# Low halves one form behind on GpSimd, one addition behind on VectorE, forms made at named places, and a broadcast copy moved from VectorE to ScalarE

## The chip, the cores and the metric

The kernel runs on one core of one Trainium2 chip. The metric is device microseconds for one execution of the whole program, as a median of runs. The engines are named as in the profile: PE is TensorE's matmul (PEld its weight load), DVE is VectorE, ACT is ScalarE, POOL is GpSimd, SP is the queue that issues the DMAs. Each engine works through its own queue in order and waits for the others through semaphores.

## What is computed

Block-causal attention over 4 batches, 8 heads, 576 positions, then a mixture of experts whose gate is balanced by eight rounds of row and column normalisation, then a soft mixture of experts:

```
x = attention(q, k, v)                      # 2304 x 512
logits = x @ w_gate
P = exp(logits - logits.max())
for _ in range(8):
    P /= P.sum(1, keepdims=True) + 1e-9
    P /= P.sum(0, keepdims=True) + 1e-9
    P *= N / E
for e in range(8):
    h = maximum(x @ w1[e], 0)               # 512 -> 1024
    out += P[:, e:e+1] * (h @ w2[e])        # 1024 -> 512
return soft_moe(out, phi, m2w1, m2w2)
```

## The kernel before

A product in full precision is made of three matmuls on rounded operands: high by high, high by low, low by high, where the high half is a rounded copy made by ACT and the low half is the source minus that copy, made by DVE or POOL. So each operand has two halves, and the low half waits for the high one.

The 8 experts are cut into 32 units u of 256 hidden columns each. Units 0 to 3 run between the attention steps. While unit 4 runs, sums and differences of the tokens are built once (`rec`, `lin`, `form`). From unit 5 on, layer 1 for the four token chunks of 512 is done by a fast multiplication: 26 products instead of 32, each of a token form with a weight form, and sums of the products. The list `IR` sets the order of these 26 products and of the copies and additions that belong to them; every product goes to one of six PSUM banks. The last chunk of 256 tokens goes the plain way (`L1P`, chunk 4, 24 matmuls of 256 columns).

Weight forms: a unit has 26, numbered k. The first 8 are blocks of the raw weight tile `r1`; the other 18 are a sum or difference made by POOL in a scratch tile (`st`, `st2`). `make()` makes the next one of the queue `aq`: POOL's sum (L902, for k of 8 and over), ACT's high half (L903), POOL's low half (L904). It is called after every piece of layer 1 (`inter` calls it while `MAIN` is set), eight times at a hook, and by `wt_of` when a product needs a form that is not there. The calls pin the order on POOL and on ACT (`keep`).

One unit goes so: the 26 products (`L1S`, matmuls at L963) are interleaved with pieces of layer 2 of the unit before and of chunk 4. Layer-2 pieces are three matmuls at L203, and a bank of six of them is added to the output by DVE at L213 (`acc`). ACT copies banks at L966, DVE adds a bank to a work tile at L970, POOL adds two work tiles, also at L970. A "fin" step makes the two halves of a hidden tile through `hsplit`: ACT's relu at L923, DVE's low half at L924. Then come layer 2 of chunks 0 and 1, and the next unit. The raw w2 tile is split by ACT (L120) and DVE (L121) in the same stretch.

The gate: `gmax_a` finds the maximum of each partition, spreads it over 128 columns (L303), PE transposes that, and `gmax_b` takes the maximum and the exponential and goes on into the first normalisation:

```
nc.vector.tensor_reduce(out=m1, in_=o[:, 0:128], axis=AX.X, op=ALU.max, negate=True)   # L308
nc.scalar.activation(out=P, in_=P, func=AF.Exp, bias=m1, scale=1.0)                    # L309
nc.vector.tensor_reduce(out=rs, in_=P, axis=AX.X, op=ALU.add)                          # L313
nc.vector.tensor_scalar(out=rs, in0=rs, scalar1=1e-9, scalar2=None, op0=ALU.add)       # L314
nc.vector.reciprocal(out=rs, in_=rs)                                                   # L315
nc.vector.tensor_tensor(out=P, in0=P, in1=rs..., op=ALU.mult)                          # L316
nc.vector.tensor_reduce(out=cs, in_=P..., axis=AX.X, op=ALU.add)                       # L317
```

The next column sum (L322, on PE) needs `cs`. At that time POOL builds the token sums: 48 additions of 128 by 512 (L795).

Of the kernel before, what the change touches and what calls it, by code (L numbers as in the profile page):

```python
# [10 lines left out]
AF = mybir.ActivationFunctionType  # L11
# [18 lines left out]
def f32(ap):  # L30
    return ap.bitcast(F32)
# [3 lines left out]
def attn_moe_softmoe_kernel(ctx: ExitStack, tc: tile.TileContext, qk1, q, k, v, wg, w1, w2, phi, m2w1, m2w2, cst, out):  # L35
# [264 lines left out]
    def gmax_a():  # L300
        nc.vector.tensor_reduce(out=m1, in_=P, axis=AX.XY, op=ALU.max)
        mbt[0] = wp.tile([128, 128], F32, tag="r", name="mbg", bufs=RB)
        nc.vector.tensor_copy(out=mbt[0], in_=m1.to_broadcast([128, 128]))  # L303

    def gmax_b():
        o = bank("gm")
# [476 lines left out]
    k = 0  # L783
# [7 lines left out]
    def keep(ins):  # L791
        tc.keep_in_program_order(ins)
# [44 lines left out]
    def raw_w2(u):  # L837
        def f():
            e, fq = divmod(u, F // FQ)
            pool, tag = (pb, "hC1") if u == 4 else (wp, "r")  # L840
            rw2[u] = pool.tile([128, 2, DM], F32, tag=tag, name="r2")
            nc.sync.dma_start(out=rw2[u], in_=w2[e, fq * FQ:(fq + 1) * FQ, :].rearrange("(k p) f -> p k f", p=128))
        return [f]

    def split_w2(u):
        i = ND + u - 4

        def new():
            wslot[i % 2] = (None, None) + tuple(wp.tile([128, 2, DM], F32R, tag=f"{n_}{i % 2}", name=n_) for n_ in ("w2h", "w2l"))
            wraw[i % 2] = (None, rw2[u])  # L850
            split_piece(i, 4)
        return [new] + [lambda pc=pc: split_piece(i, pc) for pc in range(5, 8)]
# [22 lines left out]
    def unit(u, k):  # L875
        return rw[u][:, k % 4, 128 * (k // 4):128 * (k // 4) + 128]

    def forms_of(u, plain, last):
        for k in range(26):
            n = PA.count(k) * (not plain) + (k < 8) * (5 if plain else 1)  # L880
            if n:
                eu[u, k] = n
                aq.append((u, k))

    def make():
        if not aq or not efree:
            return
        u, k = aq.pop(0)
        q = efree.pop(0)
        h, lo = entry(q)  # L890
        ew[u, k] = (h, lo, q)
        if k < 8:
            src = unit(u, k)
        else:
            if not tmpw:
                tmpw.extend([const.tile([128, 512], F32, tag="wgx", name="st"), const.tile([128, 128], F32, name="st2")])
            d, ka, a, kb, b, o = AT[k - 8]

            def tv(j):
                return tmpw[j // 4][:, 128 * (j % 4):128 * (j % 4) + 128]  # L900
            src = tv(d)
            keep(nc.gpsimd.tensor_tensor(out=src, in0=unit(u, a) if ka == "u" else tv(a), in1=unit(u, b) if kb == "u" else tv(b), op=ALU.add if o == "+" else ALU.subtract))  # L902
        keep(nc.scalar.activation(out=h, in_=src, func=AF.Copy))  # L903
        keep(nc.gpsimd.tensor_tensor(out=lo, in0=src, in1=f32(h), op=ALU.subtract))  # L904

    def make_all(u):
        while aq and aq[0][0] == u:
            assert efree
            make()

    def wt_of(u, k):
        while (u, k) not in ew:
            assert efree
            make()
        return ew[u, k][0:2]

    def used(u, k):
# [4 lines left out]
    def hsplit(h, lo, src, pin=False):  # L922
        p = [nc.scalar.activation(out=h, in_=src, func=AF.Relu)]  # L923
        p.append(nc.vector.scalar_tensor_tensor(out=lo, in0=src, scalar=0.0, in1=f32(h), op0=ALU.max, op1=ALU.subtract))  # L924
        for x in p if pin else ():
            keep(x)
# [7 lines left out]
    def L1S(u, hb):  # L934
        bk, wk = {}, {}

        def v(q):
            if q[0] == "b":
                return bk[q[1]]
            _, t, f, k = q  # L940
            if t == 4:
                return w4
            if (t, k) not in wk:
                p, g = HT[t][k == "l"]
                wk[t, k] = p.tile([128, 2, H_], F32, tag=g, name="wk")
            return wk[t, k][:, f]
        r = []
        for o in IR + [("mm",)]:
            if o[0] == "y":
                yield  # L950
            elif o[0] == "mm":
                if r:
                    yield
                if len(o) == 1:
                    break
                r.append(o)
                _, n, b, st = o
                if st:
                    bk[b] = pm2.tile([128, 512], F32, tag=f"n{b}", name="s")
                wh, wl = wt_of(u, PA[n])  # L960
                xhv, xlv = XF[n]
                for m, (a, x) in enumerate(((wh, xhv), (wh, xlv), (wl, xhv))):
                    nc.tensor.matmul(bk[b], a, x, start=(st and m == 0), stop=(m == 2), skip_group_check=not st)  # L963
                used(u, PA[n])
            elif o[0] == "copy":
                keep(nc.scalar.activation(out=v(("s",) + o[1]), in_=v(o[2]), func=AF.Copy, scale=float(o[3])))  # L966
            elif o[0] in ("add", "addb"):
                out_ = v(("s",) + o[1]) if o[0] == "add" else bk[o[1]]
                ps_ = o[2][0] == "b" or o[3][0] == "b"
                keep((nc.vector if ps_ else nc.gpsimd).tensor_tensor(out=out_, in0=v(o[2]), in1=v(o[3]), op=ALU.add if o[4] == "+" else ALU.subtract))  # L970
            else:
                t, f = o[1]
                if t not in hb:
                    hb[t] = h_new(t, F32R, "hf")
                hsplit(hb[t][0][:, f], hb[t][1][:, f], v(o[2]), True)

    def L1P(c, u, hs):
        hh, hl = hs
        n = CH[c]
        for f in range(2):  # L980
            o = bank("l1")
            for kt in range(KD):
                wh, wl = wt_of(u, 4 * f + kt)
                xhv, xlv = xs(xh, c, kt), xs(xl, c, kt)
                nc.tensor.matmul(o[:, 0:n], wh, xhv, start=(kt == 0), stop=False)
                nc.tensor.matmul(o[:, 0:n], wh, xlv, start=False, stop=False)
                nc.tensor.matmul(o[:, 0:n], wl, xhv, start=False, stop=(kt == KD - 1))
                used(u, 4 * f + kt)
                if kt == KD - 1:
                    hsplit(hh[:, f, 0:n], hl[:, f, 0:n], o[:, 0:n])  # L990
                yield

    def inter(g1, pend, pat, at=None, part=False):
        g2 = (y for x in pend for y in L2(*x))
        n = 0
        for ch in pat:
            next(g1 if ch == "p" else g2, None)
            if ch == "p":
                pop_side()
                if MAIN[0]:  # L1000
                    make()
                n += 1
                for f in (at or {}).get(n, ()):
                    f()
        for g in (g2,) if part else (g2, g1):
            for _ in g:
                pass
# [29 lines left out]
    for j, x in enumerate(["3", "2", "1", "0", "4"]):  # L1037
        if j == 1:
            while side:
                pop_side()  # L1040
        h = (hB, hA)[(j + (pend[0][2] == hB if j == 0 else flip)) % 2]
        if j == 0:
            flip = int(pend[0][2] == hB)
        n2 = 2 * (ITEM[pend[0][1]][2] // 128)
        inter(L1P(int(x), 4, h), pend, PP[n2])
        pend = [(ND, x, h)]
        if x != "4":
            assert len(gated) == NC_
            aux.extend(batch(int(x)))
        if j == 2:  # L1050
            aux.extend(raw_w2(5) + split_w2(5) + dma_w1(5))
    drain()
    apace[0] = 1
    MAIN[0] = 1
# [22 lines left out]
    for u in range(5, NU - 1):  # L1077
        i = ND + u - 4
        h4 = h_new(0, F32R, "h4")
        if u > 5:  # L1080
            inter(L1P(4, u, h4), [(i - 1, "2", hb[2])], "llll" + "p" * 8 + "llll")
            late_ = [(i - 1, "3", hb[3])]
        else:
            inter(L1P(4, u, h4), pend, "ll" + PP[4].replace("l", "", 2))
            late_ = []
        at = {17: [lambda: make_all(u)] + raw_w2(u + 1)}
        after = dma_w1(u + 1)[0]

        def l2s(hb):
            for c in range(2):  # L1090
                yield from L2(i, str(c), hb[c])
        hb = stage_s(
            u, [(i, "4", h4)] + late_, "lplplplp" + ("plppl" * 3 + "plplp" + "p" * 10 if late_ else "p" * 22), at,
            l2s, "llllyllyllyllyl", {2: split_w2(u + 1), 15: [after] + [make] * 8},
        )

    u = NU - 1
    last_i = ND + u - 4
    lp = last_i % 2
    for _ in L2(last_i - 1, "2", hb[2]):  # L1100
        pass
    h4 = []

    def last_p(hb):
        t = pb.tile([128, 2, 2, 256], F32R, tag="T12", name="h4")
        h4.extend([t[:, 0], t[:, 1]])
        return L1P(4, u, h4)
    hb = stage_s(u, [(last_i - 1, "3", hb[3])], "plppl" * 4 + "p" * 14, {}, last_p, "ppppypypypypp", {})
    assert not aq and not aux

    A = const.tile([128, DM], F32, tag="wgx", name="A")
# [405 lines left out]
```

## Time and profile before

| | |
|---|---|
| median of 3 runs | 2041.64 us (2039.04 to 2050.18) |
| profiled execution: its time, its span | 2047.44 us, 2045.7 us |
| busy: PE, DVE, POOL, ACT | 1835.8, 1229.0, 1016.5, 787.6 us |
| longest shares of the chain that ended last | PE 32%, POOL 28%, DVE 21%, issue 10%, ACT 7% |
| POOL low halves and sums in that chain (L904, L902) | 11% and 8% |
| load of a raw weight tile (512 KB), issue to landing | 3.4 us |

Busy time is the share of the span in which an engine had something to do; a busy PE is not a PE at its peak. In the chain that ended last each piece of work is followed back to what released it, so its shares tell who was waited for, not who was busy.

### The profile page before, as it was taken

Reading aid. Unit: us, or ns where it says so; the run is one execution under the profiler, and the core shown is the slowest. Engines: PE = TensorE matmul, PEld = TensorE weight load, DVE = VectorE, ACT = ScalarE, POOL = GpSimd, SP = SyncE. Lnnn points to the kernel's source line nnn. Section 1 sums busy time; section 2 is a strip of 40 time slices with the busy share of each in tenths; the row PEclk is TensorE's granted clock in tenths of the full one; section 3 lists DMA queues with packets and bytes.
Section 4 is the critical chain, followed back from the end, with each engine's and each line's share of the span. In section 5 each row is a group of like instructions: output and inputs, shape, how many; then the busy total and the mean of one; then the engine's idle time right before and its main releaser. Section 6 shows DMA issues by size and latency. Waiting matters only on the chain.

```text
span 2045.7 us, 27013 instructions
## 1 busy us (share of the span) xinstructions
PE 1835.8 (90%) x9138; PEld 1368.5 (67%) x9138; DVE 1229.0 (60%) x2286; ACT 787.6 (39%) x2196; POOL 1016.5 (50%) x1706
## 2 busy tenths in 40 slices
PE   9999998399788889888989899889888889988897
PEld 5666666387566667666767677667666667666563
DVE  6565555876566666666666666666666666666442
ACT  6666552135333333333333333333333333333332
POOL 4332225711555565566665555555555555555511
PEclk9999999699899999999999999999999999999999
DMA  5333210010000000000000000000000000000687
GB/s 200 105 103 95 66 54 11 21 52 1 21 21 21 21 21 21 21 22 21 12 21 21 21 21 13 20 21 21 21 21 21 21 21 21 21 21 22 227 280 248
DMA packets 79066, 103.14 MB, mean 50 GB/s; under 512 B 4688, under 2 KB 55632, under 8 KB 78928
## 3 DMA queue, kind: packets, MB, share of 16 engines
q1 hardware_dynamic: 78928, 101.42, 14.8%
q8 instruction: 73, 1.20, 0.2%
q14 instruction: 65, 0.53, 0.1%
HBM read 96.68 MB, written 4.72 MB: 50 GB/s over the span
## 4 chain that ended last, share of the span: by engine, by line
PE 32%; POOL 28%; DVE 21%; issue 10%; ACT 7%; POOLq 0%; DMA 0%; ACTq 0%; DVEq 0%
PE l L203 13%; POOL es L904 11%; POOL st L902 8%; POOL wk L970 5%; DVE s L970 5%; DVE wk L970 4%; DVE acc L213 4%; POOL w L970 3%; DVE hf L924 3%; ACT hf L923 3%; DVE w2l L121 2%; PE pvp L531 2%; DVE mbg L303 2%; PE tp L499 2%; PE s L417 2%
## 5 line engine op out<-in xcount | busy, mean ns | idle before, releaser
L203 PE MATMUL l<-w2h,hf 128*128 128x512 f32 x1728 | 588.6, 395 | 9.3 <-DVE acc L213 7.5
L963 PE MATMUL s<-xh,es 128*128 128x512 f32 x864 | 340.9, 416 | 63.5 <-DVE hf L924 28.1
L970 POOL TENSOR_TENSOR wk<-wk 128x512 f32<-128x512 f32 x189 | 244.4, 1311 | 305.1 <-DVE wk L970 305.0
L213 DVE SCALAR_TENSOR_TENSOR acc<-l,P,acc 128x512 f32<-128x512 f32 x504 | 362.9, 743 | 54.9 <-PE l L203 54.8
L203 PEld LDWEIGHTS l<-w2h,hf 128*128 128x128 f32 x1728 | 324.9, 188 | 95.6 <-DVE acc L213 18.5
L203 PE MATMUL l<-w2l,hf 128*128 128x512 f32 x864 | 338.0, 391 | 0.0
L904 POOL TENSOR_TENSOR es<-st,es 128x128 fp32r<-128x128 f32 x486 | 223.6, 460 | 211.6 <-ACT es L903 205.1
L903 ACT ACTIVATE es<-st 128x128 fp32r<-128x128 f32 x486 | 150.9, 311 | 456.8 <-POOL st L902 454.9
L963 PE MATMUL s<-T,es 128*128 128x512 f32 x810 | 229.0, 408 | 48.6 <-DVE wk L970 41.7
L963 PEld LDWEIGHTS s<-xh,es 128*128 128x128 f32 x864 | 165.4, 192 | 149.4 <-DVE hf L924 48.9
L923 ACT ACTIVATE hf<-s 128x512 fp32r<-128x512 f32 x189 | 110.1, 597 | 396.1 <-DVE s L970 241.5
L970 DVE TENSOR_TENSOR wk<-s,wk 128x512 f32<-128x512 f32 x216 | 148.4, 687 | 156.9 <-POOL wk L970 55.2
L963 PEld LDWEIGHTS s<-T,es 128*128 128x128 f32 x810 | 149.2, 192 | 107.2 <-DVE wk L970 59.3
L203 PEld LDWEIGHTS l<-w2l,hf 128*128 128x128 f32 x864 | 162.6, 188 | 30.8
L963 PE MATMUL s<-xl,es 128*128 128x512 f32 x432 | 172.1, 398 | 0.0
L904 POOL TENSOR_TENSOR es<-r,es 128x128 fp32r<-128x128 f32 x224 | 95.7, 464 | 144.2 <-ACT es L903 144.2
L924 DVE SCALAR_TENSOR_TENSOR hf<-s,hf 128x512 fp32r<-128x512 f32 x189 | 129.9, 688 | 43.6 <-ACT hf L923 40.8
L970 DVE TENSOR_TENSOR wk<-wk,s 128x512 f32<-128x512 f32 x81 | 55.7, 688 | 126.1 <-POOL w L970 90.4
L970 DVE TENSOR_TENSOR s<-s,wk 128x512 f32<-128x512 f32 x162 | 111.8, 690 | 26.0 <-POOL wk L970 23.1
L475 POOL TENSOR_SCALAR pe<-pe,sm 128x384 f32<-128x384 f32 (+2 forms) x80 | 54.1, 680 | 142.3 <-DVE sm L462 64.0
L203 PE MATMUL l<-w2h,h 128*128 128x512 f32 x216 | 87.4, 406 | 30.4 <-ACT h L923 16.3
L924 DVE SCALAR_TENSOR_TENSOR h<-l,h 128x256 fp32r<-128x256 f32 x54 | 22.9, 424 | 149.1 <-ACT h L923 149.1
(247 smaller groups left out, 3189.3 us busy)
## 6 DMA issues: line engine op xcount, KB each, us to landing
r<-in_moe_w_dram SPq DMA_DIRECT2D x80, 512.0 KB, 3.4
mw<-in_moe_w_dram SPq DMA_DIRECT2D x64, 512.0 KB, 6.4
kraw<-in_k_dram SPq DMA_DIRECT2D x16, 576.0 KB, 4.1
qraw<-in_q_dram SPq DMA_DIRECT2D x16, 320.0 KB, 4.7
v<-in_v_dram SPq DMA_DIRECT2D x16, 256.0 KB, 3.1
out_dram<-ob SPq DMA_DIRECT2D x6, 512.0 KB, 4.0
out_dram<-ob SPq DMA_DIRECT2D x6, 256.0 KB, 2.3
qk<-in_qk_dram SPq DMA_DIRECT2D x4, 256.0 KB, 4.4
```

What stands on the lines that cost most here:

```text
L121: p.append((nc.gpsimd if pc % (2 if i >= ND_ - 2 else WPM) == 0 and (i < WPU or ND_ - 2 <= i <= ND_) else nc.vector).tensor_tensor(out=lo, ...
L203: nc.tensor.matmul(o, lh, w[:, kf, :], start=(m == 0), stop=(m == 5))
L213: nc.vector.scalar_tensor_tensor(out=av, in0=o, scalar=P[:, tt, e:e + 1], in1=av, op0=ALU.mult, op1=ALU.add)
L303: nc.vector.tensor_copy(out=mbt[0], in_=m1.to_broadcast([128, 128]))
L475: nc.gpsimd.tensor_scalar(out=p_[:, 0:n_], in0=p_[:, 0:n_], scalar1=sm[:, i:i + 1], scalar2=1.0, op0=ALU.mult, op1=ALU.mult)
L902: keep(nc.gpsimd.tensor_tensor(out=src, in0=unit(u, a) if ka == "u" else tv(a), in1=unit(u, b) if kb == "u" else tv(b), op=ALU.add if o == ...
L903: keep(nc.scalar.activation(out=h, in_=src, func=AF.Copy))
L904: keep(nc.gpsimd.tensor_tensor(out=lo, in0=src, in1=f32(h), op=ALU.subtract))
L923: p = [nc.scalar.activation(out=h, in_=src, func=AF.Relu)]
L924: p.append(nc.vector.scalar_tensor_tensor(out=lo, in0=src, scalar=0.0, in1=f32(h), op0=ALU.max, op1=ALU.subtract))
L963: nc.tensor.matmul(bk[b], a, x, start=(st and m == 0), stop=(m == 2), skip_group_check=not st)
L970: keep((nc.vector if ps_ else nc.gpsimd).tensor_tensor(out=out_, in0=v(o[2]), in1=v(o[3]), op=ALU.add if o[4] == "+" else ALU.subtract))
```

## The change

1. `gmax_a` makes the spread copy on ACT.
2. `make()` no longer makes the low half at once. It notes it in `owed`; the next `make()` puts it behind its own sum. `wt_of`, `make_all` and a scratch tile that is needed again put out what is owed.
3. The "fin" step of `L1S` puts ACT's relu out and notes the low half in `late`; it is put out behind the next addition from a bank, or ahead of a product that opens a bank.
4. `inter` calls `make()` where the pattern has an "m", no longer after every piece of layer 1. Around chunk 4 the calls stand between pieces of layer 2 and none stands between its eight pieces of layer 1; unit 5's first eight forms are queued in unit 4. The split of chunk 4 is pinned in its place, and the hook that loads the next raw w1 stands at piece 3 instead of 15.

```diff
     def gmax_a():
-        nc.vector.tensor_copy(out=mbt[0], in_=m1.to_broadcast([128, 128]))
+        nc.scalar.activation(out=mbt[0], in_=m1.to_broadcast([128, 128]), func=AF.Copy)
...
+    owed = []
+    def flush_lo():
+        while owed:
+            out_, src_, h_, _ = owed.pop(0)
+            keep(nc.gpsimd.tensor_tensor(out=out_, in0=src_, in1=f32(h_), op=ALU.subtract))
     def make():
...
+            if any(x[3] == d for x in owed):
+                flush_lo()
             keep(nc.gpsimd.tensor_tensor(out=src, in0=unit(u, a) if ka == "u" else tv(a), in1=unit(u, b) if kb == "u" else tv(b), op=ALU.add if o == "+" else ALU.subtract))
+        flush_lo()
         keep(nc.scalar.activation(out=h, in_=src, func=AF.Copy))
-        keep(nc.gpsimd.tensor_tensor(out=lo, in0=src, in1=f32(h), op=ALU.subtract))
+        owed.append((lo, src, h, d))
...
+            if o[0] == "y" or len(o) == 1 or o[0] == "mm" and o[3]:
+                flush()
...
                 keep((nc.vector if ps_ else nc.gpsimd).tensor_tensor(out=out_, in0=v(o[2]), in1=v(o[3]), op=ALU.add if o[4] == "+" else ALU.subtract))
+                if ps_:
+                    flush()
...
-                hsplit(hb[t][0][:, f], hb[t][1][:, f], v(o[2]), True)
+                h_ = hb[t][0][:, f]
+                keep(nc.scalar.activation(out=h_, in_=v(o[2]), func=AF.Relu))
+                flush()
+                late.append((hb[t][1][:, f], v(o[2]), h_))
...
-                    hsplit(hh[:, f, 0:n], hl[:, f, 0:n], o[:, 0:n])
+                    hsplit(hh[:, f, 0:n], hl[:, f, 0:n], o[:, 0:n], MAIN[0])
...
-                if MAIN[0]:
-                    make()
...
+        if j == 3:
+            aux.extend([make] * 8)
...
-            inter(L1P(4, u, h4), [(i - 1, "2", hb[2])], "llll" + "p" * 8 + "llll")
+            inter(L1P(4, u, h4), [(i - 1, "2", hb[2])], "lmlmlml" + "p" * 8 + "lmlmlmlm")
...
-            l2s, "llllyllyllyllyl", {2: split_w2(u + 1), 15: [after] + [make] * 8},
+            l2s, "llllyllyllyllyl", {2: split_w2(u + 1), 3: [after], 15: [make] * 8},
```

How instructions move is seen in the order of the built program, for one unit in the middle. On POOL, in the stretch in which chunk 4 is at work, before (`es` are the weight forms, `r1` the raw tile, `st` the scratch tile):

```order
L902 TENSOR_TENSOR st_5498<-r1_9209 128x128
L904 TENSOR_TENSOR es0_4990<-st_5498,es0_4990 128x128 [waits PE_49,Activation_49]
L902 TENSOR_TENSOR st2_5499<-r1_9209 128x128
L904 TENSOR_TENSOR es1_5025<-st2_5499,es1_5025 128x128 [waits PE_49,Activation_49]
L902 TENSOR_TENSOR st_5498<-st2_5499,r1_9209 128x128
L904 TENSOR_TENSOR es0_4990<-st_5498,es0_4990 128x128 [waits PE_49,Activation_49]
```

The same place after the change:

```order
L912 TENSOR_TENSOR st_5462<-r1_9164 128x128
L890 TENSOR_TENSOR es3_5405<-st_5462,es3_5405 128x128 [waits PE_49,Activation_49]
L912 TENSOR_TENSOR st2_5463<-r1_9164 128x128
L890 TENSOR_TENSOR es0_4990<-st_5462,es0_4990 128x128 [waits PE_49,Activation_49]
L912 TENSOR_TENSOR st_5462<-st2_5463,r1_9164 128x128 [waits Pool_49]
L890 TENSOR_TENSOR es1_5024<-st2_5463,es1_5024 128x128 [waits PE_49,Activation_49]
```

Each low half now belongs to the sum before the one in front of it: a sum stands between a sum and its low half.

On ACT, around the second relu of chunk 4 (`h4<-l1`), before:

```order
L903 ACTIVATE es0_4990<-st_5498 128x128 [waits Pool_49]
L903 ACTIVATE es1_5025<-st2_5499 128x128 [waits Pool_49]
L903 ACTIVATE es0_4990<-st_5498 128x128 [waits Pool_49]
L903 ACTIVATE es3_5474<-st_5498 128x128 [waits Pool_49]
L923 ACTIVATE h4_9247<-l1_9292 128x256 [waits PE_49]
L903 ACTIVATE es1_5025<-st2_5499 128x128 [waits Pool_49]
```

After:

```order
L914 ACTIVATE es3_5405<-st_5462 128x128 [waits PE_49,Pool_49] x2
L937 ACTIVATE h4_9246<-l1_9273 128x256 [waits PE_49]
L937 ACTIVATE h4_9246<-l1_9288 128x256 [waits PE_49]
L914 ACTIVATE es0_4990<-st_5462 128x128 [waits Pool_49]
L914 ACTIVATE es1_5024<-st2_5463 128x128 [waits Pool_49]
L914 ACTIVATE es0_4990<-st_5462 128x128 [waits Pool_49]
```

The relu has moved ahead of four or more high halves that wait for POOL.

On DVE, where the first hidden tiles of a unit are finished (`s` are banks, `wk` work tiles, `hf` halves of a hidden tile, `w2l` the low half of w2), before:

```order
L970 TENSOR_TENSOR s_9058<-s_9058,wk_8957 128x512 [waits PE_49]
L121 TENSOR_TENSOR w2l_9151<-r2_9087,w2h_9150 128x256 [waits Activation_49] x2
L924 SCALAR_TENSOR_TENSOR hf_9094<-s_9058,hf_9093 128x512 [waits Activation_49]
L970 TENSOR_TENSOR s_8927<-s_8927,wk_8916 128x512 [waits PE_49]
L924 SCALAR_TENSOR_TENSOR hf_9094<-s_8927,hf_9093 128x512 [waits Activation_49]
L970 TENSOR_TENSOR s_9106<-s_9106,wk_8916 128x512 [waits DVE_49,PE_49]
L924 SCALAR_TENSOR_TENSOR hf_9112<-s_9106,hf_9111 128x512 [waits Activation_49]
```

After:

```order
L992 TENSOR_TENSOR s_9057<-s_9057,wk_8953 128x512 [waits PE_49]
L121 TENSOR_TENSOR w2l_9151<-r2_9087,w2h_9150 128x256 [waits Activation_49] x2
L992 TENSOR_TENSOR s_8923<-s_8923,wk_8912 128x512 [waits PE_49,Pool_49]
L967 SCALAR_TENSOR_TENSOR hf_9094<-s_9057,hf_9093 128x512 [waits Activation_49]
L967 SCALAR_TENSOR_TENSOR hf_9094<-s_8923,hf_9093 128x512 [waits Activation_49]
L992 TENSOR_TENSOR s_9106<-s_9106,wk_8912 128x512 [waits DVE_49,PE_49]
L967 SCALAR_TENSOR_TENSOR hf_9112<-s_9106,hf_9111 128x512 [waits Activation_49]
```

The second addition has moved ahead of the first low half; the third low half still follows its own addition, since a product that opens a bank comes first.

## Rows read from the trace of the kernel before

**Rows 1.** Busy time by stretch: us, each engine's busy time (x instructions), clock, DMA

```profile
360.00:380.00 20.00, 0.00 (x0) 0.00 (x0) 20.00 (x1) 0.00 (x0) 20.00 (x17) 0.50 0.00 0
...
639.79:1863.74 1223.95, 1103.19 (x4832) 852.31 (x4831) 755.81 (x1174) 429.93 (x1150) 707.58 (x1220) 1.00 0.06 20
```

**Rows 2.** Chain that ended last, first and last of its 25 such pieces

```profile
586.57 2.53 POOL wk L970 x2
...
1863.74 2.53 POOL wk L970 x2
```

**Rows 3.** Timeline of one unit, PE: start, us, instruction, idle before and releaser

```profile
1015.64 0.97 PE L963 MATMUL s<-T,es 128*128 128x512 f32 x3 [1.67 <-DVE wk L970]
1022.37 0.50 PE L963 MATMUL s<-xh,es 128*128 128x512 f32 x1 [0.20 <-DVE hf L924]
1024.33 0.50 PE L963 MATMUL s<-xh,es 128*128 128x512 f32 x1 [0.99 <-DVE hf L924]
...
1046.41 0.47 PE L203 MATMUL l<-w2h,h 128*128 128x512 f32 x1 [1.17 <-DVE acc L213]
...
1055.76 0.50 PE L963 MATMUL s<-xh,es 128*128 128x512 f32 x1 [0.22 <-ACT wk L966]
...
1061.61 0.50 PE L963 MATMUL s<-xh,es 128*128 128x512 f32 x1 [0.79 <-DVE wk L970]
```

**Rows 4.** Timeline of the same unit, POOL

```profile
1035.51 3.40 POOL L904 TENSOR_TENSOR es<-r,es 128x128 fp32r<-128x128 f32 x8 [3.37 <-ACT es L903]
...
1062.13 0.47 POOL L902 TENSOR_TENSOR st<-r,st 128x128 f32<-128x128 f32 x1
1063.01 0.46 POOL L904 TENSOR_TENSOR es<-st,es 128x128 fp32r<-128x128 f32 x1 [0.42 <-ACT es L903]
1063.43 0.47 POOL L902 TENSOR_TENSOR st<-r,st 128x128 f32<-128x128 f32 x1
```

**Rows 5.** Timeline of the same unit, ACT

```profile
1044.57 0.31 ACT L903 ACTIVATE es<-st 128x128 fp32r<-128x128 f32 x1 [0.98 <-POOL st L902]
1044.78 0.37 ACT L923 ACTIVATE h<-l 128x256 fp32r<-128x256 f32 x1
...
1060.25 0.58 ACT L966 ACTIVATE wk<-s 128x512 f32<-128x512 f32 x1
...
1064.14 0.61 ACT L966 ACTIVATE wk<-wk 128x512 f32<-128x512 f32 x1
```

**Rows 6.** Timeline of the same unit, DVE

```profile
1014.89 0.69 DVE L970 TENSOR_TENSOR wk<-s,wk 128x512 f32<-128x512 f32 x1 [1.97 <-POOL wk L970]
...
1018.35 1.92 DVE L121 TENSOR_TENSOR w2l<-r,w2h 128x256 fp32r<-128x256 f32 x2
...
1020.79 0.74 DVE L121 TENSOR_TENSOR w2l<-r,w2h 128x256 fp32r<-128x256 f32 x2
...
1023.58 0.69 DVE L924 SCALAR_TENSOR_TENSOR hf<-s,hf 128x512 fp32r<-128x512 f32 x1 [0.66 <-ACT hf L923]
...
1036.64 2.72 DVE L213 SCALAR_TENSOR_TENSOR acc<-l,P,acc 128x512 f32<-128x512 f32 x4
```

**Rows 7.** Waits of PE in units 5 and 31: total us, times, longest

```profile
PE s L963 <- ACT es L903: 8.1, 4, 2.9
...
PE s L963 <- ACT es L903: 5.2, 6, 1.9
```

**Rows 8.** Timeline around the gate's maximum, DVE, POOL and PE

```profile
350.02 38.92 DVE L303 COPY mbg<-m 128x128 f32<-128x128 f32 x1
...
388.93 2.62 POOL L795 TENSOR_TENSOR wT<-wT,wT 128x512 f32<-128x512 f32 x2
389.08 0.44 PE L307 MATMUL gm<-ident,mbg 128*128 128x128 f32 x1 [38.29 <-DVE mbg L303]
...
390.68 0.91 DVE L314 TENSOR_SCALAR rs<-rs 128x18 f32<-128x18 f32 x1
```

**Rows 9.** Line L314 in all: duration ns min/median/max, first and last start

```profile
L314 DVE TENSOR_SCALAR rs<-rs x8: 167/178/911, 390.7 to 445.5; 128x18 f32<-128x18 f32 x8
```

More of the change, by code (lines that the diff above doesn't have):

```diff
@@ L893, in make @@
             src = unit(u, k)
+            d = None
         else:
@@ L909, in make_all @@
             make()
+        flush_lo()
     def wt_of(u, k):
@@ L914, in wt_of @@
             make()
+        if any(x[2] is ew[u, k][0] for x in owed):
+            flush_lo()
         return ew[u, k][0:2]
@@ L947, in L1S, with flush @@
         r = []
+        late = []
+        def flush():
+            while late:
+                lo_, src_, h_ = late.pop(0)
+                keep(nc.vector.scalar_tensor_tensor(out=lo_, in0=src_, scalar=0.0, in1=f32(h_), op0=ALU.max, op1=ALU.subtract))
         for o in IR + [("mm",)]:
+            if o[0] == "y" or len(o) == 1 or o[0] == "mm" and o[3]:
+                flush()
             if o[0] == "y":
@@ L996, in inter @@
         for ch in pat:
+            if ch == "m":
+                make()
+                continue
             next(g1 if ch == "p" else g2, None)
@@ L1080, in attn_moe_softmoe_kernel @@
         if u > 5:
-            inter(L1P(4, u, h4), [(i - 1, "2", hb[2])], "llll" + "p" * 8 + "llll")
+            inter(L1P(4, u, h4), [(i - 1, "2", hb[2])], "lmlmlml" + "p" * 8 + "lmlmlmlm")
             late_ = [(i - 1, "3", hb[3])]
         else:
-            inter(L1P(4, u, h4), pend, "ll" + PP[4].replace("l", "", 2))
+            inter(L1P(4, u, h4), pend, "ll" + PP[4].replace("l", "", 2).replace("p", "pm"))
             late_ = []
@@ L1092, in attn_moe_softmoe_kernel @@
         hb = stage_s(
-            u, [(i, "4", h4)] + late_, "lplplplp" + ("plppl" * 3 + "plplp" + "p" * 10 if late_ else "p" * 22), at,
-            l2s, "llllyllyllyllyl", {2: split_w2(u + 1), 15: [after] + [make] * 8},
+            u, [(i, "4", h4)] + late_, ("lplplplp" + ("plppl" * 3 + "plplp" + "p" * 10 if late_ else "p" * 22)).replace("p", "pm"), at,
+            l2s, "llllyllyllyllyl", {2: split_w2(u + 1), 3: [after], 15: [make] * 8},
         )
@@ L1100, in attn_moe_softmoe_kernel @@
     for _ in L2(last_i - 1, "2", hb[2]):
-        pass
+        make()
     h4 = []
@@ L1107, in last_p @@
         return L1P(4, u, h4)
-    hb = stage_s(u, [(last_i - 1, "3", hb[3])], "plppl" * 4 + "p" * 14, {}, last_p, "ppppypypypypp", {})
+    hb = stage_s(u, [(last_i - 1, "3", hb[3])], ("plppl" * 4 + "p" * 14).replace("p", "pm"), {}, last_p, "ppppypypypypp", {})
     assert not aq and not aux
```

## The prediction

> **What bounds the kernel now.** I read the stretches first. In the main one (units 9 to 31) PE is busy 1103 of 1224 us, far ahead of DVE (756), POOL (708) and ACT (430) [rows 1]. That looks like a PE bound, but matmuls are pipelined and a busy PE may be starting late. The chain of waits gives the rhythm: the same piece, two wide POOL additions, stands in it 25 times from 586.57 to 1863.74, so a unit takes 1277.17 / 24 = 53.2 us [rows 2]. The timeline of PE for one such unit shows where it stood idle: 1.67 + 0.20 + 0.99 + 1.17 + 0.22 + 0.79 = 5.0 us, each before a product or a layer-2 piece [rows 3]. So about a tenth of a unit can be had, and not more: five of the six waits end on DVE, one on ACT, and the question is who makes DVE and ACT late.
>
> The answer stands on POOL and ACT. Where scratch forms are made, POOL does a sum (0.47 us), waits 0.42 for ACT's high half, then does the low half; sums follow each other every 1.30 us [rows 4]. ACT meanwhile stands idle 0.98 us for the next sum, and everything behind that high half in its queue stands too: the relu of chunk 4, done at once when the high half is through, and the bank copies at 1060.25 and 1064.14 [rows 5]. That makes PE wait at three places, always through one DVE step: the accumulation behind chunk 4's low half (1046.41), a copied bank (1055.76), and a sum with a copied bank (1061.61). The longest wait, 1.67 us at product 15, ends a chain of ACT copy, DVE sum, two POOL additions and a last DVE sum; its DVE sum stood 1.97 us for POOL [rows 3, 6]. The two waits for `hf` belong to the layer output.
>
> **Lows one form behind, and named places.** With another sum between a sum and its low half, ACT's copy (0.31 us) fits beside the sum. POOL's operations then follow each other at the pace that its gapless run of lows shows, 3.40 / 8 = 0.42 us, so a form costs 0.84 instead of 1.30 [rows 4, 5].
>
> First, chunk 4. The relu now stands ahead of the waiting high halves, as the order shows; it needs only its bank (0.37 [rows 5]), and the low half behind it, half the size of an `hf` one (0.69 [rows 6]), takes 0.4. Twelve layer-2 matmuls, 2.7 us at 1103.19 / 4832 = 0.23 each [rows 1], lie between that bank and the matmul at 1046.41: cover enough. Gained: 1.17 [rows 3].
>
> Second, the way from there to product 15, walked in the old clock. POOL gains 0.4 to 0.5 per form. The bank copied at 1055.13 is copied as soon as ACT is through with one high half, and the 0.22 goes. The copy of 1060.25 starts at 1058.2, its DVE sum at 1058.8, ends at 1059.5, and the product at 1061.61, due at 1060.8, starts on time: the 0.79 goes. DVE then accumulates once (0.68) and makes the next sum from 1060.2 to 1060.9; ACT's copy of it, behind one high half, runs at 1061.4 instead of 1064.14 [rows 5]. From there nothing changes its length: DVE 0.69, two POOL additions 2.53, DVE 0.69 [rows 2, 6]. So product 15 starts 2.74 us earlier, at 1066.1. PE would get there at 1068.86 - 1.67 - 0.22 - 0.79 = 1066.2 with no wait before it, or up to 1 us earlier (my allowance: a restarted PE loses a little that these idle times do not count), so a wait of up to 1 us may stay there. Gained 2.7; the lower bound is 0.2 (the next DVE wait takes all but the smallest), the upper 3.7 (all of 0.22, 0.79, 1.67, and 1.0 of restarts).
>
> **Named places and the earlier load.** The same number of forms is made. Load and hook: the raw tile's DMA is issued after piece 3, but it overwrites nothing before the last user is through, lands 3.4 us later, and the gapless lows start at 1035.51, long after; nothing waits for it, so 0. If it were late, the first lows would be, and the run of lows has slack of its own: its high halves wait for POOL.
>
> **Layer output on DVE.** The 0.99 us wait at 1024.33 follows a low half that itself waited 0.66 for ACT's relu [rows 3, 6]. With the addition ahead of the low half, that wait is covered. But the first low half then comes one addition (0.69) later, so its bank is free 0.6 later for the product that opens it, the second bank 0.6 earlier, and the third low half keeps its old place. Also, the last form's low half now runs on POOL behind its wide additions, and can stretch DVE's split of w2, which takes 1.92 for two beside POOL and 0.74 without [rows 6]: up to 0.6 more per instruction. I take 0.1 gained, bounds -0.5 and +0.6.
>
> Per unit: 1.17 + 2.7 + 0.1 = 4.0, bounds about 1 and 5.5. Over 24 units 96.
>
> **Units 5 and 31.** In unit 5, built while forms are not ahead, PE waits 8.1 us for high halves (four times), in unit 31 5.2 (six times) [rows 7]. Unit 5's first eight forms are now queued in unit 4, and unit 31's are made between the pieces of layer 2 before it. I take 8 and 5; bounds 2 to 13 (a restart included) and 0 to 8.
>
> **The gate's copy.** DVE's copy of 128 by 128 began at 350.02 and took 38.92 us, while POOL was busy 20.00 of 20 us with its additions, PE did nothing, and the transposing matmul waited 38.29 [rows 1, 8]. On ACT I price the copy at 0.31, an equal block [rows 5]. So at first sight 38 us are won. But look one step on. The maximum, the exponential and a row sum come 2 us later, then L314, a DVE instruction on SBUF alone like the copy. It took 911 ns where POOL's last addition was still at work (388.93 + 2.62 = 391.55; L314 ended 390.68 + 0.91 = 391.59) and 178 ns in the median of its eight calls [rows 8, 9]. It behaved like the copy: it stood until POOL stopped. So it will start near 352 and stand until about 391, and the column sum gets its data no earlier than before: 0, bounds -1 and +2 (PE's few matmuls that now come earlier, and a restart at half clock, 0.50 [rows 1]).
>
> The Trainium skill, "SBUF — State Buffer", section "Who interferes with whom", says that a DVE copy or tensor_scalar in a two-port mode and GpSimd exclude each other, and that whoever starts first holds the ports for its whole instruction. By its letter L314 would wait only for the addition in progress, about 1.3 us, and the edit would give some 36 us. The row speaks against one instruction as the length of the lock: the copy stood through some thirty additions.
>
> **Sum.** 96 + 8 + 5 + 0 = 109. From the profiled execution 2047.4 - 109 = 1938.4; it was 5.8 above the median, so 2041.6 - 109 = 1932.6, say 1932.
>
> **Rivals.**
> *The gate's stall goes as well.* If L314 waits for one addition only (1.3), or falls into a gap between two, 36 to 38 us more go: 1932 - 37 = 1895. For it: nothing shows L314 starting against a long run of POOL. Against it: the copy and the 911 ns. 0.11.
> *Other waits step in.* Each DVE step that comes earlier meets the next one in its queue; PE keeps the 1.17 and little else, 2 us per unit with 48, and 8 for unit 5, 5 for unit 31 gone or halved: 2041.6 - 48 - 8 - 5 = about 1980. For it: two waits for `hf` and one for product 15 are not made by the pitch [rows 3]. Against: the walk finds the 0.22 and 0.79 covered with 1 us to spare. 0.18.
> *POOL without gaps holds DVE.* The change turns POOL's paired stretches into gapless ones, sixteen operations of 0.42, 6.7 us. If DVE's accumulations stood against them as L314 did, PE would run on through the empty banks (a bank is 6 matmuls of 0.23, 1.4 us; there are six banks) and then stand: with five empty banks nothing is lost; with only one empty bank 6.7 - 1.4 = 5.3 us a unit, 1.3 more than the gain of 4.0, so 24 x 1.3 = 31 slower and, less the 13 of units 5 and 31, about 2060 (with fewer than two empty banks it decides). Against it: beside POOL's gapless run of eight lows four accumulations took 2.72, 0.68 each, as elsewhere [rows 4, 6]. 0.04.
> *The forms gain nothing in time,* since POOL's waiting only moves to another place of the same queue: within 0.5%, 0.04.
>
> **How the numbers follow.** The forecast has 0.63; with its bounds per unit of 3 and 5 it runs from 1908 to 1957. The range reaches to the first two rivals, 1888 to 1985, and leaves out some 0.15. Half a per cent, about 10 us, is about what a measurement of this kernel can tell from no change: faster 0.92, same 0.04, slower 0.04.
>
> **What would show it.** The repeated piece of the chain stands 49.2 us apart instead of 53.2; POOL's sums of forms come every 0.84 us; PE has no wait for an accumulation at the start of chunk 4's layer 2, and one of about 1 us at product 15; the accumulations stay at 0.68. Around 352 a DVE instruction of about 38 us, L314 by name, stands where the copy stood, and PE is idle until about 391. I am wrong if that instruction is short (then 37 us more go), if the period stays over 51 us with waits at the same products, or if DVE's accumulations grow beside POOL.

## The result and the profile after

1897.82 us, median of 4 runs (1897.20 to 1899.63), against 2040.7 for the kernel before: ratio 0.9292, 95% interval 0.9263 to 0.9322, 143 us less. The forecast was 1932, with 1888 to 1985 as its range. The measured time stands close to the first rival's 1895, but that rival did not happen: the gate's stall is still there, and the units and the stages around them gave the rest. The forecast's own bounds, 1908 to 1957, were missed by 10 us; the measured time lies inside the range because the range had been stretched to take in that rival.

The chain of waits of the kernel after shows the rhythm; the piece that stood 25 times in [rows 2] again stands 25 times from its first to the last one shown here:

```profile
566.13 2.55 POOL wk L992 x2
...
1727.58 2.55 POOL wk L992 x2
```

(1727.58 - 566.13) / 24 = 48.39 us a unit instead of 53.22. So the span of 2045.7 became 1895.3 like this: 20.4 up to the first piece (586.57 to 566.13), 115.7 in the 24 periods (1277.17 to 1161.45), 14.2 behind the last (181.96 to 167.72); together 150.4, of the profiled execution.

The timelines around the gate's maximum in the kernel after, ACT, DVE, POOL and PE, answer to [rows 8]:

```profile
350.67 0.31 ACT L303 ACTIVATE mbg<-m 128x128 f32<-128x128 f32 x1 [0.47 <-DVE m L301]
...
352.91 36.81 DVE L314 TENSOR_SCALAR rs<-rs 128x18 f32<-128x18 f32 x1
...
387.21 1.26 POOL L795 TENSOR_TENSOR whD<-wT,whD 128x512 f32<-128x512 f32 x1
388.43 1.26 POOL L795 TENSOR_TENSOR whC<-wT,whC 128x512 f32<-128x512 f32 x1
389.76 2.61 POOL L795 TENSOR_TENSOR wT<-wT,wT 128x512 f32<-128x512 f32 x2
...
391.69 0.59 PE L322 MATMUL cs<-cs,ones 128*128 128x8 f32 x2 [37.22 <-DVE cs L317]
```

The copy costs 0.31 on ACT, and an instruction on 18 numbers per partition then takes 36.81 us on DVE. Where PE had waited 38.29 for the copy it now waits 37.22 for the column sums. L314 ends at 352.91 + 36.81 = 389.72. POOL's additions overlap by a few hundredths (388.43 starts before 387.21 + 1.26 ended), up to the one that ends at 389.69; the next starts at 389.76. In that hole of 0.07 us L314 ends.

The timelines of PE, POOL and ACT for one unit after answer to [rows 3 to 5]:

```profile
1005.13 0.96 PE L985 MATMUL s<-T,es 128*128 128x512 f32 x3 [0.67 <-DVE wk L992]
1012.27 0.51 PE L985 MATMUL s<-xh,es 128*128 128x512 f32 x1 [0.24 <-DVE hf L967]
1017.51 0.50 PE L203 MATMUL l<-w2h,hf 128*128 128x512 f32 x1 [0.29 <-DVE hf L967]
1053.37 0.97 PE L985 MATMUL s<-T,es 128*128 128x512 f32 x3 [0.66 <-DVE wk L992]
...
1032.73 0.46 POOL L912 TENSOR_TENSOR st<-st,r 128x128 f32<-128x128 f32 x1
1033.14 0.47 POOL L890 TENSOR_TENSOR es<-st,es 128x128 fp32r<-128x128 f32 x1
1033.56 0.47 POOL L912 TENSOR_TENSOR st<-st 128x128 f32<-128x128 f32 x1
...
1030.21 0.39 ACT L937 ACTIVATE h<-l 128x256 fp32r<-128x256 f32 x1 [0.65 <-PE l L1014]
```

Of six waits three are left from product 15 to the next product 15, with 0.24 + 0.29 + 0.66 = 1.2 us in place of 5.0. This is the shorter of two kinds of unit that alternate; in the other, one more product waits 0.39 for a low half made by POOL:

```profile
1058.70 0.73 PE L985 MATMUL s<-xh,es 128*128 128x512 f32 x2 [0.39 <-POOL es L890]
```

POOL's sums follow each other after 0.83 (1032.73, 1033.56) instead of 1.30, and chunk 4's relu waits for PE alone.

How much of the gain was idle time is read from the groups of PE's instructions in the main stretch of 23 units (busy time, mean ns | idle time before). Before:

```profile
L203 PE MATMUL l<-w2h,hf 128*128 128x512 f32 x1473 | 499.5, 394 | 6.9 <-DVE acc L213 6.9
...
L963 PE MATMUL s<-xh,es 128*128 128x512 f32 x736 | 285.6, 410 | 46.7 <-DVE hf L924 23.8 <-DVE wk L970 18.2 <-ACT wk L966 4.6
L963 PE MATMUL s<-T,es 128*128 128x512 f32 x691 | 193.8, 405 | 40.4 <-DVE wk L970 38.3
...
L203 PE MATMUL l<-w2h,h 128*128 128x512 f32 x184 | 74.0, 402 | 26.8 <-ACT h L923 14.0 <-DVE acc L213 12.9
```

After:

```profile
L203 PE MATMUL l<-w2h,hf 128*128 128x512 f32 x1472 | 502.9, 393 | 10.5 <-DVE hf L967 7.4 <-DVE acc L213 0.9
...
L985 PE MATMUL s<-xh,es 128*128 128x512 f32 x736 | 277.7, 403 | 11.0 <-DVE hf L967 5.9 <-POOL es L890 4.3
L985 PE MATMUL s<-T,es 128*128 128x512 f32 x691 | 185.9, 393 | 15.3 <-DVE wk L992 15.3
...
L203 PE MATMUL l<-w2h,h 128*128 128x512 f32 x184 | 71.6, 389 | 0.0
```

Idle time fell from 120.8 to 36.8, 84.0 us or 3.65 a unit. And the busy time fell, by the stretches, from 1103.19 [rows 1] to

```profile
614.68:1727.58 1112.90, 1076.16 (x4831) 856.69 (x4830) 762.05 (x1174) 420.22 (x1150) 699.31 (x1219) 1.00 0.07 23
```

1076.16: 27.0 us or 1.17 a unit, for the same matmuls at the same clock. 3.65 + 1.17 = 4.82, the whole gain of a unit. Every wait costs more than its idle time, as the neighbours of the matmul at 1061.61 in [rows 3] show, by the timeline of PE before:

```profile
1060.20 0.39 PE L203 MATMUL l<-w2l,hf 128*128 128x512 f32 x1
1060.43 0.39 PE L203 MATMUL l<-w2h,hf 128*128 128x512 f32 x1
...
1061.94 0.40 PE L963 MATMUL s<-xl,es 128*128 128x512 f32 x1
```

Without a wait each of these matmuls is 0.39 long, but the next starts after 0.23 (1060.20, 1060.43), inside it. Here the starts stand 1.18 apart (1060.43, 1061.61), so 0.95 is lost where the profile counts 0.79 of idle time; and the first matmul after the wait is 0.50 long, with the next one 0.33 behind it (1061.94) instead of 0.23. Together 1.05 for 0.79.

### The profile page after: what moved, and what is told of

It reads as the page before. It is cut to its first block, busy times and chain, and to the rows that moved or that the text cites. A ratio compares the mean times of both kernels' runs of the same rounds, so it can differ in the third digit from the quotient of the medians.

```text
span 1895.3 us, 27087 instructions
## 1 busy us (share of the span) xinstructions
PE 1793.0 (95%) x9138; PEld 1370.7 (72%) x9138; DVE 1235.2 (65%) x2285; ACT 777.1 (41%) x2197; POOL 1006.9 (53%) x1706
## 3 DMA queue, kind: packets, MB, share of 16 engines
q8 instruction: 72, 1.18, 0.3%
## 4 chain that ended last, share of the span: by engine, by line
PE 57%; DVE 19%; POOL 10%; ACT 6%; issue 5%; DMA 1%; POOLq 0%; ACTq 0%; DVEq 0%; SPq 0%
PE l L203 27%; PE s L985 10%; POOL wk L992 5%; DVE s L992 5%; DVE wk L992 4%; DVE acc L213 3%; PE pvp L531 2%; ACT wk L988 2%; PE tp L499 2%; DVE rs L314 2%; PE s L417 2%; DVE hf L967 2%; DVE w2l L121 2%; POOL st L912 2%; ACT hf L1000 2%
## 5 line engine op out<-in xcount | busy, mean ns | idle before, releaser
L213 DVE SCALAR_TENSOR_TENSOR acc<-l,P,acc 128x512 f32<-128x512 f32 x504 | 369.3, 745 | 118.2 <-PE l L203 115.2
L203 PEld LDWEIGHTS l<-w2h,hf 128*128 128x128 f32 x1728 | 324.3, 188 | 103.1 <-DVE hf L967 20.4
L985 PE MATMUL s<-xh,es 128*128 128x512 f32 x864 | 325.9, 403 | 16.3 <-POOL es L890 6.9
L890 POOL TENSOR_TENSOR es<-st,es 128x128 fp32r<-128x128 f32 x486 | 229.0, 471 | 71.4 <-ACT es L914 71.4
L985 PE MATMUL s<-T,es 128*128 128x512 f32 x810 | 217.8, 394 | 20.1 <-DVE wk L992 18.2
L985 PEld LDWEIGHTS s<-xh,es 128*128 128x128 f32 x864 | 160.6, 188 | 81.9 <-DVE hf L967 23.1
L988 ACT ACTIVATE wk<-s 128x512 f32<-128x512 f32 x189 | 105.8, 589 | 34.6 <-PE s L985 34.6
L120 ACT ACTIVATE w2h<-r 128x256 fp32r<-128x256 f32 x160 | 54.2, 406 | 107.9 <-PE l L203 70.0
```

The lines of the kernel that those rows point to most:

```text
L120: p = [nc.scalar.activation(out=h, in_=r[:, a:a + 256], func=AF.Copy)]
L203: nc.tensor.matmul(o, lh, w[:, kf, :], start=(m == 0), stop=(m == 5))
L213: nc.vector.scalar_tensor_tensor(out=av, in0=o, scalar=P[:, tt, e:e + 1], in1=av, op0=ALU.mult, op1=ALU.add)
L890: keep(nc.gpsimd.tensor_tensor(out=out_, in0=src_, in1=f32(h_), op=ALU.subtract))
```

## The experiments

The first four do one part of the change alone, on the kernel before; e5 and e6 leave a part out. The times per unit are worked out from the starts of PE's matmuls number 3045 and 8085, 24 units of 210 apart; before 53.22.

| kernel | median us | ratio (95% interval) | us a unit |
|---|---|---|---|
| e1 copy on ACT | 2047.82 | 0.9996 (0.9987 to 1.0005) | 53.29 |
| e2 lows behind | 1936.68 | 0.9448 (0.9432 to 0.9464) | 49.16 |
| e3 late lows | 2021.15 | 0.9864 (0.9849 to 0.9879) | 52.41 |
| e4 named places | 2015.87 | 0.9836 (0.9822 to 0.9851) | 52.43 |
| e5 no late lows | 1906.55 | 0.9318 (0.9304 to 0.9332) | 48.64 |
| e6 no places | 1919.63 | 0.9380 (0.9366 to 0.9394) | 48.64 |
| the change | 1897.82 | 0.9292 (0.9263 to 0.9322) | 48.39 |
| e7 norm forms | 1901.79 | 0.9291 (0.9277 to 0.9305) | 48.50 |
| e8 written order | 1869.50 | 0.9136 (0.9120 to 0.9151) | 48.39 |
| e9 column sum +2 | 1864.77 | 0.9113 (0.9099 to 0.9127) | 48.20 |
| e10 column sum +3 | 1865.29 | 0.9113 (0.9098 to 0.9128) | 48.20 |

The kernel before took 2049.53 beside e1 to e4, 2047.32 beside e5 to e8 and 2046.88 beside e9 and e10; gains in us below are against these, and kernels measured beside different ones are compared by their ratios.

**e1, the copy alone.**

```diff
-        nc.vector.tensor_copy(out=mbt[0], in_=m1.to_broadcast([128, 128]))
+        nc.scalar.activation(out=mbt[0], in_=m1.to_broadcast([128, 128]), func=AF.Copy)
```

> The kernel before with the broadcast copy on ScalarE and nothing else. My theory: the copy takes about 0.3 us, and L314 stands in its place, from about 352 to the first moment at which POOL pauses in its run of additions, some 37 us; ratio 0.998 to 1.002. Rival, the lock lasts one instruction of POOL: L314 under 1.5 us, 36 us less, ratio 0.982.

No gain, and the timeline has L314 in the copy's place:

```profile
353.26 36.92 DVE L314 TENSOR_SCALAR rs<-rs 128x18 f32<-128x18 f32 x1
...
388.88 1.26 POOL L795 TENSOR_TENSOR whC<-wT,whC 128x512 f32<-128x512 f32 x1
390.22 2.61 POOL L795 TENSOR_TENSOR wT<-wT,wT 128x512 f32<-128x512 f32 x2
```

It ends at 390.18, again in the hole, between 390.14 and 390.22.

**e2, POOL's lows one behind alone.**

```diff
-        keep(nc.gpsimd.tensor_tensor(out=lo, in0=src, in1=f32(h), op=ALU.subtract))
+        owed.append((lo, src, h, d))     # put out by the next make(), behind its sum
```

> The kernel before with POOL's low halves one form behind and nothing else; make() is still called after every piece of layer 1. My theory: POOL's forms follow each other every 0.84 us, the waits at 1055.76 and 1061.61 go and the one at product 15 shrinks, but high halves still stand ahead of chunk 4's relu, so that PE's wait for an accumulation at the start of chunk 4's layer 2 stays in part: 2.7 to 3.5 us a unit, 65 to 85 us in all, ratio 0.958 to 0.968. Rival, the pace of the forms is not what holds PE, the places are: under 1 us a unit, ratio over 0.985.

113 us, 4.06 a unit: more than expected, and 84% of a unit's whole gain. What is left on PE in a unit:

```profile
1023.78 0.96 PE L977 MATMUL s<-T,es 128*128 128x512 f32 x3 [0.64 <-DVE wk L984]
1032.54 0.50 PE L977 MATMUL s<-xh,es 128*128 128x512 f32 x1 [0.98 <-DVE hf L938]
1041.20 0.50 PE L203 MATMUL l<-w2h,hf 128*128 128x512 f32 x1 [0.29 <-DVE acc L213]
```

The waits at 0.22 and 0.79 are gone, product 15's is 0.64, and chunk 4's 1.17 has gone as well (averaged over 24 units 0.94 of the 1.33 by which the starts stood apart there), although the relu still stands among the high halves: those now come through in time. The pace of the forms held PE.

**e3, VectorE's late lows alone.**

```diff
-                hsplit(hb[t][0][:, f], hb[t][1][:, f], v(o[2]), True)
+                keep(nc.scalar.activation(out=h_, in_=v(o[2]), func=AF.Relu))
+                flush()
+                late.append((hb[t][1][:, f], v(o[2]), h_))
```

> The kernel before with VectorE's low halves of the layer output one addition behind and nothing else. My theory, as predicted: 0.1 us a unit, at most 0.6, ratio 0.993 to 1.001. Rival, from the trace of after, where the wait of 0.99 for hf has become 0.24: 0.7 us or more a unit, 17 us, ratio under 0.992.

28 us, 0.81 a unit: my 0.1 failed for the part alone. Averaged over the 24 units, the layer output itself takes 0.5 less: the wait of 0.99 goes, and layer-2 matmuls behind it start 0.4 and 0.3 later. The larger share, 0.9, is the wait at chunk 4 (0.72 in the unit nearest to that of [rows 3], where it was 1.17), at a place that the edit doesn't touch; 0.55 is lost again at product 7, the one that started at 1055.76 before.

**e4, the named places alone** (the calls of `make()`, the earlier load, unit 5's eight forms, chunk 4's split pinned).

```diff
-            inter(L1P(4, u, h4), [(i - 1, "2", hb[2])], "llll" + "p" * 8 + "llll")
+            inter(L1P(4, u, h4), [(i - 1, "2", hb[2])], "lmlmlml" + "p" * 8 + "lmlmlmlm")
```

> The kernel before with the calls of make() at the named places, the earlier load, unit 5's first eight forms queued in unit 4 and chunk 4's split pinned; each low half still stands right behind its sum. My theory: the wait for an accumulation at chunk 4 (1.17 us a unit) goes, and unit 5 gives 8 to 16; the pitch of the forms stays 1.30, so the waits at products 7, 11 and 15 stay: 35 to 50 us in all, ratio 0.975 to 0.983. Rival, the places are what matters: the waits at the products go too, ratio under 0.96.

33.7 us, 0.79 a unit: the ratio lies just past the end of what I expected (0.983, which its interval takes in), and the waits are the expected ones, as the timeline of PE shows:

```profile
1001.23 0.96 PE L963 MATMUL s<-T,es 128*128 128x512 f32 x3 [2.13 <-DVE wk L970]
1018.54 0.50 PE L203 MATMUL l<-w2h,hf 128*128 128x512 f32 x1 [0.30 <-DVE acc L213]
1040.08 0.50 PE L963 MATMUL s<-xh,es 128*128 128x512 f32 x1 [0.42 <-ACT wk L966]
1045.95 0.50 PE L963 MATMUL s<-xh,es 128*128 128x512 f32 x1 [0.78 <-DVE wk L970]
```

Chunk 4's 1.17 is gone, and 0.46 of it comes back at product 15 (2.13 after 1.67), because the forms still come every 1.30 us.

**e5 and e6, the change less one part.** e5 leaves out the late lows of e3, e6 the places of e4; neither has the copy on ACT, which gave nothing in e1.

> The changed kernel without VectorE's late low halves (and with the broadcast copy on VectorE again, which gave nothing alone): POOL's lows one behind and the named places. If the late lows give beside the other parts what they gave alone (0.8 us a unit, 28 us in all), the ratio is 0.938 to 0.945. Rival, as I predicted it: once POOL and ACT are in time they give 0.1 us a unit, ratio 0.929 to 0.932.

> The kernel before with POOL's lows one behind and VectorE's late lows, make() still called after every piece of layer 1. My theory: the 13 us of waits for an accumulation that are left in the stretch of 19 units when the lows alone are behind (0.6 us a unit) and unit 5's waits are what the places remove; so 25 to 40 us more than the changed kernel, ratio 0.941 to 0.949. Rival, the parts add up (113 + 28 = 141 us of the 143): the places add nothing beside the others, ratio 0.929 to 0.933.

e5 lies at the rival's end: beside the other parts the late lows give 0.25 a unit, near the 0.1 of the forecast, not 0.8. e6: the places give 0.0088 of the ratio, 18 us: 0.25 a unit as well, 6 us in the 24 periods, 8 us in unit 5 and 7 in the last units (by the profiled executions, which lie 20.7 apart). That is less than my 25 to 40 and more than the rival's nothing. Neither 0.25 is well known: kernels with the very units of the change took 48.20 to 48.50 a unit (e7 to e10 below), so the parts' shares beside each other are uncertain by about as much as they measure. Alone the parts give 4.06 + 0.81 + 0.79 = 5.66 a unit, together 4.83: whoever takes a wait away first has it.

**e7, other instruction forms in the normalisation.**

```diff
-        nc.vector.tensor_scalar(out=rs, in0=rs, scalar1=1e-9, scalar2=None, op0=ALU.add)
+        nc.vector.tensor_tensor(out=rs, in0=rs, in1=eps[:, 0:NT], op=ALU.add)
...
-            nc.vector.tensor_scalar(out=cs, in0=cs, scalar1=float(N) / E, scalar2=None, op0=ALU.mult)
-            nc.vector.tensor_tensor(out=P, in0=P, in1=cs..., op=ALU.mult)
+            nc.vector.scalar_tensor_tensor(out=P, in0=P, scalar=float(N) / E, in1=cs..., op0=ALU.mult, op1=ALU.mult)
```

> The changed kernel with the gate's normalisation in other forms on VectorE: L314 adds a tile of 1e-9 (tensor_tensor instead of tensor_scalar), and the factor N/E is taken into the multiplication behind L325 (scalar_tensor_tensor), so that no one-input instruction on SBUF alone is left in it. If the stall belongs to the one-input forms: L314 takes 0.2 to 1.5 us at 352, PE runs on, 25 to 37 us less than the changed kernel, ratio 0.911 to 0.918. Rival, any VectorE instruction that has only SBUF operands stands until POOL pauses: L314 or L316 takes 35 us or more, ratio 0.928 to 0.931.

Nothing: the timeline has the same stall under another form (L316 is L314 of the other kernels).

```profile
353.15 36.82 DVE L316 TENSOR_TENSOR rs<-rs,eps 128x18 f32<-128x18 f32 x1
...
388.67 1.26 POOL L796 TENSOR_TENSOR whC<-wT,whC 128x512 f32<-128x512 f32 x1
390.01 2.60 POOL L796 TENSOR_TENSOR wT<-wT,wT 128x512 f32<-128x512 f32 x2
```

The one-input form isn't what holds it. Reductions of an SBUF tile (0.30) and instructions of 512 columns that read PSUM (0.69) passed beside the gate's earlier additions at their usual length.

**e8, POOL's additions in written order.** In the kernels above the program puts an independent addition between any two of which one needs the other, but for the last two; pinned, they come as they are written, and splits of weights stand among them.

```diff
-        return lambda: tt(1, out=ws[d], in0=ws[a], in1=ws[b], op=...)
+        return lambda: keep(nc.gpsimd.tensor_tensor(out=ws[d], in0=ws[a], in1=ws[b], op=...))
```

> The changed kernel with POOL's 32 second additions pinned in the order in which they are written, so that splits that wait for ScalarE, and additions that need the one just ahead, stand among them and make POOL pause early. If VectorE's L314 is let in at POOL's first pause, it ends at that pause, before 375 instead of at 389.7, and the time goes down by 5 to 30 us (ratio 0.914 to 0.927); later VectorE instructions on SBUF stand until the next pauses. Rival, L314 waits for the end of the additions (or for one of them by name): it ends at 389 or later, ratio 0.929 or more.

32 us below the change by the ratios, 0.9136 against 0.9292, the intervals well apart (28 by the medians, but the kernel before took 6.6 more beside e8), and just past the 30 that I expected at most. e7, measured beside e8 and with the stall, took 32.3 more than e8. The timelines of DVE, POOL and PE:

```profile
353.22 3.96 DVE L314 TENSOR_SCALAR rs<-rs 128x18 f32<-128x18 f32 x1
...
353.42 1.29 POOL L804 TENSOR_TENSOR whC<-whC,wT 128x512 f32<-128x512 f32 x1
...
354.66 2.48 POOL L804 TENSOR_TENSOR wT<-wT,wT 128x512 f32<-128x512 f32 x2
...
357.23 1.26 POOL L804 TENSOR_TENSOR wT<-wT,wT 128x512 f32<-128x512 f32 x1
...
359.15 0.60 PE L322 MATMUL cs<-cs,ones 128*128 128x8 f32 x2 [4.37 <-DVE cs L317]
```

The fourth of these additions overwrites a tile that the third reads. It starts at 357.23, 0.09 after the third ended (354.66 + 2.48 = 357.14), and L314 ends at 357.18, in between: at the first hole, after three additions instead of thirty. PE waits 4.37 where it waited 37.22.

Later calls of the same line did not need a hole. The timelines of DVE and POOL in the same kernel, some 20 us on:

```profile
375.19 0.60 DVE L314 TENSOR_SCALAR rs<-rs 128x18 f32<-128x18 f32 x1
...
374.39 1.36 POOL L804 TENSOR_TENSOR wT<-whD,whC 128x512 f32<-128x512 f32 x1
375.71 6.67 POOL L804 TENSOR_TENSOR wT<-wT,wT 128x512 f32<-128x512 f32 x5
```

The second addition here starts (375.71) before the first has ended (375.75), and L314 ends at 375.79 all the same. Six instructions of the gate were let in so in e8, between two additions that overlap, after 0.47 to 1.34 us, and none behind the first L314 took longer. So a hole ended the long stand each time, but what made the first L314, or the copy in the kernel before, stand through boundaries of a kind at which the later ones passed is not shown.

**e9 and e10, the first column sum later** (on e8).

```diff
-    SG = [0, 2, 3, 2, 2, 3, 2, 2]
+    SG = [2, 2, 3, 2, 2, 3, 2, 2]     # e10: [3, 2, 2, 2, 2, 2, 2, 2]
```

> e8_written_order with the first column sum of the gate put two side steps later in PE's queue (12 layer-2 matmuls, 2.7 us, each). In e8 PE stood 4.37 us there behind L314's 3.96 and then ran some 5 us at half clock. My theory: 5.4 us more of cover hide the wait and its restart: 5 to 8 us less than e8, ratio 0.909 to 0.9115. Rival: the later rounds of the normalisation push a VectorE instruction into another run of POOL without pauses, and the wait comes back at a later column sum: ratio 0.913 or more.

> The same with three side steps ahead of the first column sum and one fewer ahead of the third and of the sixth, so that the last round is one step later than in e8. If the cover of the first wait is all that counts, as e9, ratio 0.909 to 0.9115; if closer column sums wait for VectorE's slower instructions beside POOL, some of it is lost, ratio 0.912 or more.

Both are the fastest measured, 0.9113, but not for the reason given: 0.19 a unit, 4.5 us, comes from the units, which these edits don't touch. In the change and in e8 units alternate between 48.2 and 48.55 to 48.6, where one product waits 0.3 to 0.4 for a POOL low half every other time; here all are 48.2, and in e7 all are 48.5. What decides between these rhythms stays open. At the gate 1 us came, since the wait is back at the next column sum of e9, by the timelines of DVE, ACT and PE:

```profile
368.17 0.69 DVE L179 SCALAR_TENSOR_TENSOR hl<-l,hh 128x512 fp32r<-128x512 f32 x1 [4.08 <-ACT hh L178]
...
366.63 1.03 ACT L120 ACTIVATE w2h<-r 128x256 fp32r<-128x256 f32 x3 [7.34 <-DMA r<-in_moe_w_dram]
...
372.47 0.56 PE L322 MATMUL cs<-cs,ones 128*128 128x8 f32 x2 [5.27 <-DVE cs L317]
```

DVE's next row sum stands behind a low half that waits for ACT, and ACT for a load of w2. That a wait returns was the rival, but its mechanism, a long VectorE instruction beside POOL, was not it.

## Why the prediction was right, and where it was not

The forecast's mechanisms held, and its sum was 41 us too small (109 for 150 in the profiled executions). That the time still lies in the range is in part luck, since the range reached below 1908 only for a rival that did not happen.

**What bounds the kernel.** Right. The pace of POOL's forms, through ACT's queue, made PE late: e2 alone takes four fifths of a unit's gain. (The stretch called units 9 to 31 runs from unit 7's piece to unit 30's; it is 23 units as counted.)

**The way to product 15.** The mechanism was right, the size too small. Forecast 2.7 and 1.17 at chunk 4; averaged over 24 units, the same matmuls stand closer by 1.33 at chunk 4, 0.47 at 1055.76, 1.43 from 1061.61 on and 1.1 before product 15, together 4.3 of 4.83. The walk was 0.3 short and chunk 4 0.16; another 0.4 lies in steps of under 0.1 each, spread over the unit. The term that I mis-sized is the restart of PE: the walk held a part of it, since it goes by starts, but chunk 4 was taken at its idle time and the rest left to the upper bound ("1.0 of restarts"), where 1.17 of a unit's gain is busy time. That makes 0.8 a unit, 115.7 for 96. Which edit has which share was off too: the 1.17 at chunk 4 was put down to the relu's new place, and e2 removes most of it without that.

**Layer output on VectorE.** 0.1 forecast; about 0.25 beside the other parts (e5, uncertain as said there), 0.8 alone (e3), where it shortens a wait that the lows behind remove anyway.

**Units 5 and 31.** Too small, 34.6 ahead of the first piece and behind the last instead of 13, and partly a slip in counting. I counted 24 periods as if they were all units; most of unit 6 lies ahead of the first piece, and parts of units 30 and 31 behind the last, worth their 4.8 a unit too. And unit 5 gave more than its waits for high halves. The middle of unit 5 by stretches, the same 107 matmuls, before:

```profile
500.20:542.11 41.91, 30.34 (x107) 20.52 (x105) 12.39 (x19) 13.45 (x38) 26.10 (x47) 0.84 0.05 13
```

and after:

```profile
500.02:529.88 29.86, 23.94 (x107) 17.76 (x105) 15.07 (x25) 12.12 (x33) 21.86 (x38) 1.00 0.07 21
```

12.05 us less, 6.4 of it busy time: the granted clock was 0.84 here, that is partly at the lower level, behind the waits, and is 1.00 now that the longest are gone.

**The gate's copy.** Right, by name and length: L314, "about 38 us" forecast, 36.81 measured, nothing gained (e1: 0.9996). By the letter of the Trainium skill, "SBUF — State Buffer", section "Who interferes with whom", VectorE would wait for the GpSimd instruction that holds the shared ports, one addition, about 1.3 us. For the first L314 the traces disagree with the length: 36.8 us through some thirty additions (e1, e7, the change), 3.96 through three (e8), each time up to the first addition that itself had to wait. For the later calls in e8 they agree: none took longer than 1.34. The 911 ns from which the forecast argued ([rows 9]) fit both readings, since one addition was still at work there; it was the copy's 38.92 that told them apart.

**The rivals.** Gapless forms on POOL didn't hold DVE's accumulations (a single one takes 0.75, as before), and other waits did not step in: 1.2 us of idle time are left of 5.0. The sum closes so: 109 forecast, 19.7 more in the periods and 21.6 more around them make 150; the medians moved 143, since the profiled execution of before lay above its median.

## What to carry to other kernels

A short operation on an in-order queue can set the pace of a whole kernel if another engine waits for its answer each time; put a second, independent operation between question and answer, and look for what else in both queues stands behind it. When idle times of TensorE are added up, add what each restart costs (here a unit gained 4.82 where 3.65 was idle time). When one stall is moved to another engine, look at the next instruction on the first engine: if its operands lie in the same memory and it meets the same neighbour, the stall may only change its line, as in e1.

## What the runs showed that was not expected

A VectorE instruction that had all its operands in SBUF, with one input (36.81) or two (36.82), stood beside a run of GpSimd additions that overlap, through some thirty of them, until the first hole of 0.07 to 0.09 us, which an addition makes that depends on the one just ahead of it. Reordering the additions so that such a pair comes early, with not one instruction more, took 32 us. Later instructions of the same kind passed between two overlapping additions after 0.47 to 1.34 us (e8), so a hole let the waiting instruction in every time, but it is not always needed; what tells the two cases apart stays open.
